# Lists of the tokens of experts two to eight: match matrices and one product in place of scatters to a table in memory

## The chip, the cores and the metric

The kernel runs on one core of a Trainium2 chip, as one program. The metric is the device time of one execution in microseconds (us), and the median of several executions is quoted. TensorE is called PE here, VectorE DVE, ScalarE ACT, GpSimd POOL; SP is the engine that issues most of the transfers. Durations of single instructions come from one profiled execution.

## The reference

Three layers follow each other: attention with two kinds of masks, a mixture of eight experts of which each token takes one, and a dense layer with a squared relu.

```
logits = x @ w_gate
e_idx = np.argmax(logits, axis=1)          # one expert per token
...
for e in range(E):
    mask = e_idx == e
    h = np.maximum(x[mask] @ w1[e], 0.0)
    ye = h @ w2[e]
    out[mask] = gate_w[mask, None] * eom[mask, e, None] * ye
...
h = np.maximum(x @ w_in, 0.0)
return (h * h @ w_out)
```

There are 2304 tokens of 512 numbers, eight experts of 512x1024x512, and a dense layer of 512x2048x512. All is float32.

## The kernel before

**Stages.** Attention runs to about 150 us, by batch and block. As it ends, tokens leave in 18 tiles of 128: each tile's rows are written to a table `x_d` in memory, and `route` finds the expert of each token and `posi`, its place in a list that gives every expert 2304 rows. Then the experts run one after the other, the largest first: the kernel calls them slots, `k` = 0 to 7, and slot `k` has `CAPS[k]` columns (416, 368, 344, ... 256). Last comes the dense layer, in three groups of six tiles, with output written by indirect transfers.

**A slot.** `e_l1(k, f)` makes a block of 128 of the 1024 inner numbers: `h` is twelve matmuls on PE. ACT takes `hh` from it (relu, rounded) and DVE `hl` (what rounding left out). `e_l2` multiplies these with the second weights: `y`, twelve matmuls a block, two blocks later. Every product of two float32 operands is three matmuls of rounded parts (`mm3`), so every weight unit of 512 KB is loaded by SP (`rw`), rounded by ACT (`hw`) and its remainder taken by DVE (`lw`, 128x1024). Five buffers hold loaded units and six hold `hw` and `lw`. In the names `hw2_0_1` the numbers are first or second weights, slot and unit.

**The tokens of a slot.** `win_load(k)` gathers the rows of slot `k` from `x_d` by an indirect transfer on POOL's queue (`win`), 128 rows at a time by a list of row numbers. `win_split` turns them on PE (`wt`), and ACT and DVE make their rounded parts `xh` and `xl`. In both orders DVE's queue holds the weight remainder `lw2_1_1` directly ahead of slot 1's first `xl1`; its buffer comes free when PE has done `y` of block 5, the last product ahead of `wt`. Slot 0's tokens and list (`lead["ix"]`) are made apart, in `match_rows` and `late_rows`, while attention ends: for each tile a 128x128 matrix says which token stands at which place modulo 128, a small operand holds tile and token number where the 128-row block is the slot's, and 13 small bfloat16 matmuls (`ips`) sum these into a list.

**The lists of slots 1 to 7.** `scatter` puts each token's number into the table `tab_d` in memory, at row `posi`: 18 indirect transfers of 128 numbers of four bytes, on POOL's queue, all after attention (`seen` holds them back until the last tile's matches are made). `rows_of` then reads a slot's list from `tab_d` into `ix`, and it waits for all scatters. The slot's expert is known from `order_slots` on DVE (`key`, `gt`, `sr`, `kk_`, `tmp`, `mf`, `meta`), which also finds offsets and surplus. `places` and 18 more indirect transfers (`idx_d`) say where each result row goes.

**What sets the order.** A scheduler lays out every engine's queue ahead of time; the engines then run their queues in that order and wait on semaphores. `tc.issue_after(x)` keeps an instruction behind `x` in that layout, and `keep_in_program_order` keeps SP's early loads in order. The parts of the weights that the dense layer needs (`e6wi`, eight-byte numbers) are loaded by SP beside the experts and converted between blocks (`conv`).

**Surplus tokens.** `overflow` handles tokens beyond `CAPS`; it stands behind a branch on `meta`, at the end.

Of the kernel before, what the change touches and what calls it, by code (L numbers as in the profile page):

```python
# [20 lines left out]
P = 128  # L21
NT = B * S
# [50 lines left out]
CONV = [(k, f) for k in range(1, 8) for f in range(8)][1:-14]  # L73
NW = (max(CAPS) + P - 1) // P
NEG = -1.0e9
# [20 lines left out]
C_TK = C_IA + P  # L96
C_END = C_TK + 2 * LATE
C_BF = C_ML - P


def make_consts():
    import numpy as np

    c = np.zeros((P, C_END), np.float32)
    p = np.arange(P)
    c[:, C_ID : C_ID + P] = np.eye(P)
    w = np.arange(KW)
    rel = (p % QB)[:, None] + STRIDE - w[None, :]
    ml = np.where((rel >= 0) & (rel < STRIDE), 0.0, NEG)
# [7 lines left out]
    c[:, C_TK:C_END:2] = np.arange(LATE)  # L117
# [14 lines left out]
def moe_kernel(ctx, tc, q, k, v, wg, wog, w1, w2, w_in64, w_out64, consts, out, dbg=None):  # L132
# [40 lines left out]
    toki = const.tile([P, NTILE, 2], I32, name="toki")  # L173
    tok1 = big.tile([P, NTILE], I32, name="tok1")

# [343 lines left out]
    late_ = []  # L519
    scat = []  # L520
    scq = []
    done = set()
# [98 lines left out]
    def match_rows():  # L621
# [9 lines left out]
        wt = wk.tile([P, LATE, 2, NW], BF16, name="wtm", tag="wtm", bufs=1)  # L631
        tk = cstb[:, C_TK - C_BF : C_END - C_BF].rearrange("p (t e) -> p t e", e=2)
        nc.vector.tensor_tensor(
# [78 lines left out]
    def late_rows(t0, t1, rows):  # L712
# [3 lines left out]
        for t in range(t0, t1):  # L716
            pm = wk.tile([P, NL], F32R, name=f"pm{t}", tag="pm", bufs=PMB)
            lead["pm"] = nc.vector.tensor_scalar(
                pm, cst[:, C_IO : C_IO + NL], rel[:, t - t0 : t - t0 + 1], None, op0=ALU.is_equal
            )  # L720
            pms.append((t, pm))
            lead["pmt"] = pm
        with tc.issue_after(lead["pm"].ins):
# [46 lines left out]
    def route(b, ts, lg, rows):  # L770
# [71 lines left out]

        def scatter(i, t):
            ins = nc.gpsimd.indirect_dma_start(  # L844
                out=tab_d[:, :],
                out_offset=bass.IndirectOffsetOnAxis(ap=posi[:, t : t + 1], axis=0),
                in_=tok1[:, t : t + 1],
                in_offset=None,
            )
            if scat:  # L850
                tc.declare_no_dep(ins.ins, group="scatter", reason="bucket rows of different tokens differ")
            tc.add_to_no_dep_group("scatter", ins.ins)
            scat.append(ins)
            return ins

        for i, t in enumerate(ts):
            scq.append(lambda i=i, t=t: scatter(i, t))

    tg = transposes(0, tiles[0])
# [6 lines left out]
    load_v(1, tiles[1])  # L866
    nc.gpsimd.memset(zero, 0)
    nc.sync.dma_start(tab_d.rearrange("(p c) o -> p (c o)", p=P), zero)
    nc.sync.dma_start(x_d[0].rearrange("(p c) -> p c", c=P), zero[: D // P, :P].bitcast(F32))
    for b in range(B):  # L870
# [60 lines left out]
    offe = r("offe", [E])  # L931

    def order_slots():
        key = r("key", [E])
# [3 lines left out]
        nc.vector.scalar_tensor_tensor(out=key, in0=lead["top"], scalar=32768.0, in1=key, op0=ALU.mult, op1=ALU.add)  # L938
        bc = lambda a: a[:, None, :].to_broadcast([P, E, E])
        bl = lambda a: a[:, :, None].to_broadcast([P, E, E])  # L940
        gt = r("gt", [E, E])
# [68 lines left out]

    def row_order_of(k):
        with tc.issue_after(lead["row"].ins):
            return nc.values_load(meta[0:1, k : k + 1], engines=[ET.Pool], min_val=0, max_val=E - 1)

    units = []
# [14 lines left out]
    def prep_unit(u):  # L1030
# [249 lines left out]
    for k in range(E):  # L1280
        for f in range(NF1):
# [188 lines left out]
    def overflow():  # L1470
# [155 lines left out]
```

## Time and profile before

| what | us |
|---|---|
| median of three executions | 814.04 (807.04 to 815.79) |
| the profiled execution | 805.34 |
| its span, first to last instruction | 803.7 |
| PE busy in it | 762.1 |
| DVE, ACT, POOL busy | 552.0, 459.4, 204.1 |

The profiled execution is 1.6 us longer than its span, and 8.7 us below the median of the three. The profile's engine shares are averages over stages: attention (to 150 us), slot 0 (150 to 209 us), slots 1 to 7 (to about 396 us) and the dense layer. PE's granted clock was 0.985 of full speed on average; where it is below 1 it is at 0.5, the lower of two levels (1.2 in place of 2.4 GHz).

### The profile page before, as it was taken

The page shows a single profiled execution, that of the slowest core. Times are in us where ns is not written, and L with a number is a line of the kernel's source. Part 1 is how long each engine was busy: PE and PEld are TensorE (multiplying, and loading weights), DVE is VectorE, ACT ScalarE, POOL GpSimd, SP SyncE. Part 2 cuts the span into 40 slices and gives each one's busy share as a digit, 9 for nine tenths or more (in the row PEclk, how much of TensorE's full clock was granted, in tenths as well). Part 3 has the DMA queues.
Part 4 walks back from the last instruction along what each step waited for, and adds up shares of the span by engine and source line. Part 5 has one row for each costly group of instructions (what it writes and reads, how often), then busy time and mean ns, then how long its engine had stood idle before and what let it go on. Part 6 is the DMA issues. An engine that isn't in the chain of part 4 may idle for free.

```text
span 803.7 us, 14547 instructions
## 1 busy us (share of the span) xinstructions
PE 762.1 (95%) x5409; PEld 681.6 (85%) x5409; DVE 552.0 (69%) x1062; ACT 459.4 (57%) x930; POOL 204.1 (25%) x193
## 2 busy tenths in 40 slices
PE   8899999993999999999999999989999999999995
PEld 4677777983999999999998889978898888899894
DVE  4777787842357587779778988897565589456533
ACT  2655646422355466566667767777565578466443
POOL 6100102744563764432013312304000003000002
PEclk9999999997899999999999999999999999999999
DMA  9799814997378998876535544454223225323002
GB/s 182 164 195 207 152 54 118 241 136 217 103 146 293 212 286 260 309 252 206 185 125 178 189 142 160 171 155 173 92 81 118 73 91 172 104 73 115 4 1 81
DMA packets 111155, 124.87 MB, mean 155 GB/s; under 512 B 40228, under 2 KB 83912, under 8 KB 111080
## 3 DMA queue, kind: packets, MB, share of 16 engines
q1 hardware_dynamic: 101256, 100.49, 46.7%
q0 software_dynamic: 8320, 22.64, 8.8%
q10 hardware_dynamic: 1504, 0.76, 0.5%
q8 instruction: 44, 0.72, 0.4%
q14 instruction: 31, 0.25, 0.1%
HBM read 101.74 MB, written 22.12 MB: 154 GB/s over the span
## 4 chain that ended last, share of the span: by engine, by line
PE 59%; issue 19%; DMA 6%; DVE 6%; POOL 5%; ACT 2%; SPq 1%; POOLq 0%; ACTq 0%; DVEq 0%
PE o L1099 5%; PE o L1100 5%; PE o L1101 5%; PE h L1099 3%; PE y L1100 3%; PE y L1099 3%; PE y L1101 3%; PE rw L551 3%; PE h L1100 3%; PE h L1101 3%; DMA tab_d<-tok,posi 2%; DMA idx_d<-toki,cpi 1%; POOL tab_d L844 1%; POOL out_dram L1361 1%; PE wt L1177 1%
## 5 line engine op out<-in xcount | busy, mean ns | idle before, releaser
L1082 DVE TENSOR_TENSOR lw<-rw,hw 128x1024 fp32r<-128x1024 f32 x62 | 79.6, 1284 | 51.8 <-ACT hw L1078 43.6
L1099 PE MATMUL o<-hwo,gh 128*128 128x512 f32 x288 | 113.8, 395 | 0.9 <-ACT gh L1331 0.9
L1100 PE MATMUL o<-lwo,gh 128*128 128x512 f32 x288 | 113.5, 394 | 0.0
L1078 ACT ACTIVATE hw<-rw 128x1024 fp32r<-128x1024 f32 x62 | 65.6, 1062 | 75.7 <-PE h L1100 51.6
L1328 ACT ACTIVATE rl<-rl 128x384 f32<-128x384 f32 x96 | 49.4, 516 | 85.4 <-DVE rl L1326 85.4
L1361 POOL DMA_INDIRECT out_dram<-ob,idx x18 | 23.6, 1311 | 251.4 <-ACT ob L1360 246.7
L1099 PE MATMUL h<-xh,hw 128*128 128x416 f32 (+7 forms) x256 | 81.3, 318 | 5.0 <-DVE hl L1206 4.9
L1101 PE MATMUL o<-hwo,gl 128*128 128x512 f32 x288 | 84.3, 396 | 0.4 <-DVE gl L1333 0.4
L1101 PE MATMUL h<-xh,lw 128*128 128x416 f32 (+7 forms) x256 | 80.1, 313 | 0.0
L1100 PE MATMUL h<-xl,hw 128*128 128x416 f32 (+7 forms) x256 | 79.9, 312 | 0.0
L1333 DVE TENSOR_TENSOR gl<-rl,gh 128x384 fp32r<-128x384 f32 x96 | 55.1, 576 | 35.0 <-ACT rl L1332 34.6
L1100 PE MATMUL y<-hl,hw 128*128 128x416 f32 (+7 forms) x256 | 77.8, 313 | 0.0
L1101 PE MATMUL y<-hh,lw 128*128 128x416 f32 (+7 forms) x256 | 77.3, 312 | 0.0
L1099 PE MATMUL y<-hh,hw 128*128 128x416 f32 (+7 forms) x256 | 66.3, 315 | 1.1 <-ACT hh L1204 1.1
L1099 PEld LDWEIGHTS o<-hwo,gh 128*128 128x128 f32 x288 | 54.1, 188 | 11.7 <-ACT gh L1331 2.2
L1100 PEld LDWEIGHTS o<-lwo,gh 128*128 128x128 f32 x288 | 54.2, 188 | 9.5
L1101 PEld LDWEIGHTS o<-hwo,gl 128*128 128x128 f32 x288 | 53.3, 188 | 9.3 <-DVE gl L1333 1.4
L1099 PEld LDWEIGHTS h<-xh,hw 128*128 128x128 f32 x256 | 48.4, 189 | 6.9 <-DVE hl L1206 6.7
L1332 ACT ACTIVATE rl<-rl 128x384 f32<-128x384 f32 x96 | 50.1, 522 | 2.2
L1331 ACT ACTIVATE gh<-rl 128x384 fp32r<-128x384 f32 x96 | 50.0, 521 | 1.9
L205 POOL TENSOR_TENSOR cvtwo<-cvtwo,cvdwo 128x512 int32<-128x512 int32 x16 | 25.6, 1607 | 94.3 <-DVE cvtwo L200 60.2
L1100 PEld LDWEIGHTS y<-hl,hw 128*128 128x128 f32 x256 | 48.8, 191 | 0.1
(614 smaller groups left out, 1935.5 us busy)
## 6 DMA issues: line engine op xcount, KB each, us to landing
rw<-in_moe_w_dram SPq DMA_DIRECT2D x62, 512.0 KB
rwa<-ws_d SPq DMA_DIRECT2D x24, 512.0 KB
rwb<-ws_d SPq DMA_DIRECT2D x24, 384.0 KB
e6wi<-in_moe_w_in_dram SPq DMA_DIRECT2D x32, 256.0 KB
rwo<-wout_d SPq DMA_DIRECT2D x16, 512.0 KB
x_d<-xr SPq DMA_DIRECT2D x18, 256.0 KB
ws_d<-eo POOLq DMA_DIRECT2D x16, 256.0 KB, 4.8
s0wo<-in_moe_w_out_dram SPq DMA_DIRECT2D x8, 512.0 KB
```

Source lines behind the costliest of these rows:

```text
L205: nc.gpsimd.tensor_tensor(t, t, rd, op=ALU.add)
L551: lead["rw"] = nc.tensor.matmul(ps[:, kk, :], xT[:, kd, col : col + P], igw[:, kd, :], start=True, stop=True)
L1078: ia = nc.scalar.activation(hi, raw, AF.Copy)
L1082: iv = eng.tensor_tensor(lo, raw, hi.bitcast(F32), op=ALU.subtract)
L1099: kept(nc.tensor.matmul(ps, ah, bh, start=first, stop=False))
L1100: kept(nc.tensor.matmul(ps, ah, bl_, start=False, stop=False))
L1101: kept(nc.tensor.matmul(ps, al, bh, start=False, stop=last))
L1328: nc.scalar.activation(rl[:, :HC], src, AF.Relu)
L1331: nc.scalar.activation(hh[:, :HC], rl[:, :HC], AF.Square)
L1332: ia = nc.scalar.activation(rl[:, :HC], rl[:, :HC], AF.Square)
L1333: iv = nc.vector.tensor_tensor(hl[:, :HC], rl[:, :HC], hh[:, :HC].bitcast(F32), op=ALU.subtract)
L1361: ins = nc.gpsimd.indirect_dma_start(out=out[:, :], out_offset=bass.IndirectOffsetOnAxis(ap=idx[:, gt_, 0:1], axis=0), in_=ob, in_offset=None,
```

## The change

The lists of slots 1 to 7 are made on the chip's engines as slot 0's list is, for all seven at once, and all scatters to `tab_d` leave the path (they stand in `overflow` now). `slot_rows` makes on DVE, from `posi` and the sorted experts, eighteen 128x128 bfloat16 match matrices (three instructions of 128x768) and an operand of 42 columns a tile (two instructions of 128x378); `end` sums eighteen matmuls of 42 columns on PE between two blocks of slot 0, and two DVE instructions make the list `rows` of 21 columns. What DVE makes lives in `y2T`, a buffer that holds results of slots later; `spots`, a load on POOL's queue, brings its constants. `order_slots` is split: what the lists need comes first, the rest (`order_rest`, `places`) after block 4. The memsets of `y2T` (`fill_sums`) come behind slot 1's gathers, and `e6wi` loads stand behind the first load of a slot-1 weight.

```diff
@@ tables, tables_end
-        nc.vector.tensor_scalar(tok1, cst[:, C_IDX : C_IDX + NTILE], 1.0, None, op0=ALU.add)
-    zero = big.tile([P, E * NT // P], I32, name="zero")
+    zero = big.tile([KD, P], F32, name="zero")
@@ before the experts
-    tab_e = tab_d.rearrange("(e r) o -> e (r o)", e=E)
-    def rows_of(k, reg):
-        ix = const.tile([P, NW], I32, name=f"ix{k}")
-        nw = (CAPS[k] + P - 1) // P
-        lead["row"] = nc.gpsimd.dma_start(ix[:, :nw], tab_e[bass.ds(reg, 1), : nw * P].rearrange("e (c p) -> p (e c)", p=P))
-        return ix
...
-        def scatter(i, t):
-            ins = nc.gpsimd.indirect_dma_start(
-                out=tab_d[:, :],
...
-    seen = wk.tile([P, 1], F32, name="seen", tag="seen", bufs=1)
-    with tc.issue_after(lead["win"].ins):
-        lead["seen"] = nc.gpsimd.tensor_copy(seen, lead["pmt"][:, 0:1].bitcast(F32))
-    with tc.issue_after(lead["seen"].ins):
-        while scq:
-            lead["row"] = scq.pop(0)()
@@ conv_load
-            nc.sync.dma_start(
...
+            with tc.issue_after(lead["w1"].ins):
+                nc.sync.dma_start(
...
@@ new
+    spots = y2T[:, 1, : C_END - C_IA]
+    nc.gpsimd.dma_start(spots, consts[:, C_IA:])
     ixs = {}
+    def slot_rows():
+        K, T = E - 1, NTILE
...
+        hi, hf, posm2, rel = new([T], I32), new([T]), new([T]), new([T, K])
+        nc.vector.tensor_scalar(hi, posi, P - 1, None, op0=ALU.bitwise_and)
+        nc.vector.tensor_copy(hf, hi)
+        nc.vector.tensor_tensor(posm2, posi, hf, op=ALU.subtract)
+        pm = y2T[:, 0, : T * P // 2].bitcast(BF16).rearrange("p (t c) -> p t c", c=P)
+        for t in range(0, T, 6):
+            sh = [P, 6, P]
+            nc.vector.tensor_tensor(
+                pm[:, t : t + 6],
+                hf[:, t : t + 6, None].to_broadcast(sh),
+                spots[:, None, :P].to_broadcast(sh),
+                op=ALU.is_equal,
+            )
+        rowb = new([E])
...
+        eq = new(sh[1:])
+        nc.vector.tensor_tensor(
+            eq,
+            rel[:, :, :, None].to_broadcast(sh),
+            cst[:, None, None, C_PJ : C_PJ + NW1].to_broadcast(sh),
+            op=ALU.is_equal,
+        )
...
+        for j in range(2):
+            nc.vector.tensor_tensor(
+                wt[:, :, j],
...
+        def end():
+            ps = psm.tile([P, 512], F32, name="rows", tag="a", bufs=6)[:, : 2 * R]
+            for t in range(T):
+                w = wt[:, t].rearrange("p j r -> p (j r)")
+                with tc.issue_after(lead["sum"].ins):
+                    nc.tensor.matmul(ps, pm[:, t], w, start=(t == 0), stop=(t == T - 1))
+            ix = const.tile([P, R], I32, name="rows")
+            nc.vector.tensor_copy(i2, ps[:, R:])
+            nc.vector.scalar_tensor_tensor(
+                out=ix, in0=ps[:, :R], scalar=float(P), in1=i2, op0=ALU.mult, op1=ALU.add
+            )
...
@@ the loop over slots and blocks
-            if f == 1 and k + 1 < E:
-                if k == 0:
-                    with tc.issue_after(lead["step"].ins):
-                        order_slots()
-                    ixs[1] = rows_of(1, row_order_of(1))
-                    fill_sums(0)
+            if (k, f) == (0, 0):
+                order_slots()
+            if (k, f) == (0, 1):
+                rows_end = slot_rows()
+            if (k, f) == (0, 3):
+                rows_end()
+            if f == (3 if k == 0 else 1) and k + 1 < E:
                 win_load(k + 1)
-                lead["row"] = lead["win"]
-                if k == 0:
-                    for d in range(1, KD):
-                        fill_sums(d)
-                if k + 2 < E:
-                    ixs[k + 2] = rows_of(k + 2, row_order_of(k + 2))
-            if (k, f) == (0, 1):
-                places()
+            if (k, f) == (0, 3):
+                for d in range(KD):
+                    fill_sums(d)
+            if (k, f) == (0, 4):
+                with tc.issue_after(lead["step"].ins):
+                    order_rest()
+                    places()
@@ overflow
+        tok1 = ov.tile([P, NTILE], I32, name="tok1")
...
+        for t in range(NTILE):
+            ins = nc.gpsimd.indirect_dma_start(
+                out=tab_d[:, :],
...
```

On POOL, from the last gather of slot 0 to what stands behind slot 1's gathers, before:

```order
L596 DMA win0_384_2051<-x_d_85,ix0_2027 32x512
L909 COPY seen_2432<-pm17_2356 128x1
L844 DMA tab_d_86<-tok1_94,posi_91 18432x1 x18
L1013 TENSOR_LOAD meta_92
L1013 ISA x2
L592 ISA
L592 DMA ix1_2586<-tab_d_86 128x3x1
L1184 MEMSET y2T_2484 128x2672
L596 DMA win1_0_2589<-x_d_85,ix1_2586 128x512
L596 DMA win1_128_2591<-x_d_85,ix1_2586 128x512
L596 DMA win1_256_2593<-x_d_85,ix1_2586 112x512
L1184 MEMSET y2T_2484 128x2672 x3
```

and now:

```order
L584 DMA win0_384_2048<-x_d_85,ix0_2024 32x512
L1156 DMA y2T_2461<-in_consts_dram 128x164
L584 DMA win1_0_2640<-x_d_85,rows_2637 128x512
L584 DMA win1_128_2642<-x_d_85,rows_2637 128x512
L584 DMA win1_256_2644<-x_d_85,rows_2637 112x512
L1153 MEMSET y2T_2461 128x2672 x4
L584 DMA win2_0_2929<-x_d_85,rows_2637 128x512
L584 DMA win2_128_2931<-x_d_85,rows_2637 128x512
```

The scatters, the reading of a register and the load of a list are gone; the load of constants stands in their place, and the first memset has moved from ahead of the gathers `win1` to behind them.

On DVE, where slot 0's first remainders `hl0_0` to `hl0_2` are taken, before:

```order
L835 TENSOR_TENSOR toki_93<-e13_2463,gsm3_2456 128x5
L836 TENSOR_TENSOR toki_93<-toki_93 128x5
L1206 SCALAR_TENSOR_TENSOR hl0_0_2528<-h0_0_2514,hh0_0_2527 128x416
L1082 TENSOR_TENSOR lw2_0_0_2500<-rw2_0_0_2496,hw2_0_0_2498 128x1024
L1206 SCALAR_TENSOR_TENSOR hl0_1_2545<-h0_1_2531,hh0_1_2544 128x416
L935 SCALAR_TENSOR_TENSOR key_2548<-cnt_2454,cst_66 128x8
L1082 TENSOR_TENSOR lw2_0_1_2506<-rw2_0_1_2502,hw2_0_1_2504 128x1024
L1206 SCALAR_TENSOR_TENSOR hl0_2_2641<-h0_2_2627,hh0_2_2640 128x416
L938 SCALAR_TENSOR_TENSOR key_2548<-top_1997,key_2548 128x8
L1082 TENSOR_TENSOR lw1_0_2_2512<-rw1_0_2_2508,hw1_0_2_2510 128x1024
```

and now (`y2T` is the place of the new lists' operands, `lw` are remainders of weight units):

```order
L1189 TENSOR_TENSOR y2T_2461<-y2T_2461 128x126
L1197 TENSOR_TENSOR y2T_2461<-y2T_2461,cst_66 128x378
L1250 SCALAR_TENSOR_TENSOR hl0_0_2506<-h0_0_2492,hh0_0_2505 128x416
L1050 TENSOR_TENSOR lw2_0_0_2478<-rw2_0_0_2474,hw2_0_0_2476 128x1024
L1181 TENSOR_TENSOR y2T_2461<-y2T_2461 128x768 x3
L1207 TENSOR_TENSOR y2T_2461<-y2T_2461 128x18x21 x2
L1050 TENSOR_TENSOR lw2_0_1_2484<-rw2_0_1_2480,hw2_0_1_2482 128x1024
L1250 SCALAR_TENSOR_TENSOR hl0_1_2536<-h0_1_2522,hh0_1_2535 128x416
L1050 TENSOR_TENSOR lw1_0_2_2490<-rw1_0_2_2486,hw1_0_2_2488 128x1024
L1250 SCALAR_TENSOR_TENSOR hl0_2_2570<-h0_2_2556,hh0_2_2569 128x416
L1050 TENSOR_TENSOR lw2_0_2_2554<-rw2_0_2_2550,hw2_0_2_2552 128x1024
L1050 TENSOR_TENSOR lw1_0_3_2654<-rw1_0_3_2650,hw1_0_3_2652 128x1024
```

New work stands ahead of `hl0_0` (its last two instructions are shown) and between the weight remainders `lw2_0_0` and `lw2_0_1`, ahead of `hl0_1`.

## Rows read from the trace of the kernel before

**Rows 1.** The page, head and part 1: span; busy time, share, instructions by engine.

```profile
span 803.7 us, 14547 instructions
...
PE 762.1 (95%) x5409; PEld 681.6 (85%) x5409; DVE 552.0 (69%) x1062; ACT 459.4 (57%) x930; POOL 204.1 (25%) x193
```

**Rows 2.** Waits of PE, whole run: engine, line, waited for: us in total, times, longest.

```profile
PE wt L1177 <- DMA win<-x_d,ix: 13.1, 1, 13.1
```

**Rows 3.** Timeline of PE, 128 to 232: start, us, engine, line, out<-in [idle before <-releaser].

```profile
133.65 0.48 PE L641 MATMUL ips<-wtm,pmh 128*128 128x8 bf16 x13
...
175.03 0.45 PE L1099 MATMUL h<-xh,hw 128*128 128x416 f32 x1 [1.80 <-DVE hl L1206]
...
199.33 1.97 PE L1177 MATMUL wt<-cst,win 128*128 128x128 f32 x8 [13.07 <-DMA win<-x_d,ix]
...
202.55 0.69 PE L1099 MATMUL y<-hh,hw 128*128 128x416 f32 x1
```

**Rows 4.** Timeline of POOL, 128 to 232, same columns.

```profile
173.95 1.37 POOL L844 DMA_INDIRECT tab_d<-tok,posi  x1 [0.30 <-issue]
188.10 0.81 POOL L592 DMA_DIRECT2D ix<-tab_d  x1 [12.78 <-DMA tab_d<-tok,posi]
...
194.45 1.04 POOL L596 DMA_INDIRECT win<-x_d,ix  x1 [3.19 <-DMA ix<-tab_d]
```

**Rows 5.** Timeline of PE, 150 to 176, same columns.

```profile
154.91 0.35 PE L1099 MATMUL h<-xh,hw 128*128 128x416 f32 x1
...
160.25 0.35 PE L1099 MATMUL h<-xh,hw 128*128 128x416 f32 x1
```

**Rows 6.** Tile tab_d: durations min/median/max in ns, first and last start; transfers' landing.

```profile
L844 POOL DMA_INDIRECT tab_d<-tok,posi x18: 967/972/2175, 145.9 to 173.9; - x18
...
DMA to landing us min/median/max: 2.5/11.2/15.6
```

**Rows 7.** Tile win, 130 to 230: the gathers' landing.

```profile
DMA to landing us min/median/max: 3.4/4.0/6.2
```

**Rows 8.** Windows: us, busy (x) by engine PE, PEld, DVE, ACT, POOL; clock, DMA, GB/s.

```profile
175.50:179.00 3.50, 3.50 (x12) 3.32 (x12) 1.23 (x1) 1.49 (x2) 0.00 (x0) 0.52 1.29 214
202.50:206.30 3.80, 3.80 (x13) 3.63 (x13) 0.79 (x2) 0.54 (x1) 3.11 (x3) 0.50 0.02 4
207.00:400.00 193.00, 189.13 (x1323) 187.22 (x1323) 137.81 (x213) 111.32 (x190) 88.43 (x90) 1.00 0.78 232
```

**Rows 9.** Waits, all engines, 130 to 240.

```profile
ACT hw L1078 <- DMA rw<-in_moe_w_dram: 21.1, 5, 8.9
```

**Rows 10.** Transfers, 168 to 173: packets and bytes moved.

```profile
DMA packets 217, 0.22 MB, mean 44 GB/s; under 512 B 4, under 2 KB 217, under 8 KB 217
```

**Rows 11.** Timeline of DVE, 128 to 232.

```profile
151.40 0.15 DVE L921 COPY cnt<-cntp 128x8 f32<-128x8 f32 x1
...
153.37 0.59 DVE L1206 SCALAR_TENSOR_TENSOR hl<-h,hh 128x416 fp32r<-128x416 f32 x1 [0.28 <-ACT hh L1204]
...
162.82 0.21 DVE L953 TENSOR_REDUCE offe<-tm 128x8 f32<-128x64 f32 x1
...
164.06 0.57 DVE L1206 SCALAR_TENSOR_TENSOR hl<-h,hh 128x416 fp32r<-128x416 f32 x1
```

**Rows 12.** Groups by form on DVE, 120 to 240: busy us, mean ns of one | idle.

```profile
L1082 DVE TENSOR_TENSOR lw<-rw,hw 128x1024 fp32r<-128x1024 f32 x18 | 22.6, 1258 | 32.2 <-ACT hw L1078 24.5 <-PE y L1101 7.7
...
L1180 DVE TENSOR_TENSOR xl<-wt,xh 128x512 fp32r<-128x512 f32 x4 | 2.7, 687 | 7.5 <-ACT xh L1179 7.5
...
L388 DVE TENSOR_TENSOR pr3l<-pr3l,rc3l 128x384 f32<-128x384 f32 x2 | 1.1, 547 | 0.0
```

**Rows 13.** Groups by form on ACT, 120 to 240.

```profile
L1078 ACT ACTIVATE hw<-rw 128x1024 fp32r<-128x1024 f32 x19 | 19.9, 1056 | 32.0 <-DMA rw<-in_moe_w_dram 21.1 <-PE h L1100 10.1 <-ACT hh L1204 0.4
```

**Rows 14.** Groups by form on POOL, whole run.

```profile
L1184 POOL MEMSET y2T<- 128x2672 f32 x4 | 9.2, 2345 | 0.0
```

**Rows 15.** Waits of ACT, 206 to 420.

```profile
ACT hw L1078 <- PE h L1100: 51.6, 22, 3.8
```

More of the change, by code (lines that the diff above doesn't have):

```diff
@@ L73 @@
 CONV = [(k, f) for k in range(1, 8) for f in range(8)][1:-14]
-NW = (max(CAPS) + P - 1) // P
+NW, NW1 = ((c + P - 1) // P for c in CAPS[:2])
 NEG = -1.0e9
@@ L96 @@
 C_TK = C_IA + P
-C_END = C_TK + 2 * LATE
+C_END = C_TK + 2 * NTILE
 C_BF = C_ML - P
@@ L116, in make_consts @@
     c[:, C_IA:C_TK] = np.arange(P)
-    c[:, C_TK:C_END:2] = np.arange(LATE)
+    c[:, C_TK:C_END:2] = np.arange(NTILE)
     c[:, C_TK + 1 : C_END : 2] = p[:, None] + 1
@@ L173, in moe_kernel @@
     toki = const.tile([P, NTILE, 2], I32, name="toki")
-    tok1 = big.tile([P, NTILE], I32, name="tok1")
     def tables():
@@ L519, in moe_kernel @@
     late_ = []
-    scat = []
-    scq = []
     done = set()
@@ L631, in match_rows @@
         wt = wk.tile([P, LATE, 2, NW], BF16, name="wtm", tag="wtm", bufs=1)
-        tk = cstb[:, C_TK - C_BF : C_END - C_BF].rearrange("p (t e) -> p t e", e=2)
+        tk = cstb[:, C_TK - C_BF : C_TK - C_BF + 2 * LATE].rearrange("p (t e) -> p t e", e=2)
         nc.vector.tensor_tensor(
@@ L721, in late_rows @@
             pms.append((t, pm))
-            lead["pmt"] = pm
         with tc.issue_after(lead["pm"].ins):
@@ L841, in route @@
             weigh()
-        def scatter(i, t):
-            ins = nc.gpsimd.indirect_dma_start(
-                out=tab_d[:, :],
[L846 to L857, printed above, removed]
     tg = transposes(0, tiles[0])
@@ L866, in moe_kernel @@
     load_v(1, tiles[1])
-    nc.gpsimd.memset(zero, 0)
-    nc.sync.dma_start(tab_d.rearrange("(p c) o -> p (c o)", p=P), zero)
-    nc.sync.dma_start(x_d[0].rearrange("(p c) -> p c", c=P), zero[: D // P, :P].bitcast(F32))
+    nc.gpsimd.memset(zero, 0.0)
+    nc.sync.dma_start(x_d[0].rearrange("(p c) -> p c", c=P), zero)
     for b in range(B):
@@ L931, in moe_kernel @@
     offe = r("offe", [E])
+    srt = {}
+    bc = lambda a: a[:, None, :].to_broadcast([P, E, E])
+    bl = lambda a: a[:, :, None].to_broadcast([P, E, E])
     def order_slots():
@@ L938, in order_slots @@
         nc.vector.scalar_tensor_tensor(out=key, in0=lead["top"], scalar=32768.0, in1=key, op0=ALU.mult, op1=ALU.add)
-        bc = lambda a: a[:, None, :].to_broadcast([P, E, E])
-        bl = lambda a: a[:, :, None].to_broadcast([P, E, E])
         gt = r("gt", [E, E])
@@ L950, in order_slots, with order_rest @@
         nc.vector.tensor_copy(meta[:, :E], mf[:, 0])
+        srt.update(gt=gt, kk=kk_)
+    def order_rest():
+        gt, kk_ = srt["gt"], srt["kk"]
         tm2 = r("tm2", [E, E])
@@ L1009, in order_of @@
         return oreg[k]
-    def row_order_of(k):
-        with tc.issue_after(lead["row"].ins):
-            return nc.values_load(meta[0:1, k : k + 1], engines=[ET.Pool], min_val=0, max_val=E - 1)
     units = []
@@ L1072, in prep_unit @@
             lead["raw"] = nc.sync.dma_start(raw, src)
+            if kind == "w1" and c == 0:
+                lead["w1"] = lead["raw"]
         nwh[0] += 1
@@ L1100, in mm3 @@
         kept(nc.tensor.matmul(ps, ah, bl_, start=False, stop=False))
-        kept(nc.tensor.matmul(ps, al, bh, start=False, stop=last))
+        lead["sum"] = kept(nc.tensor.matmul(ps, al, bh, start=False, stop=last))
     halves = [(kd, c, i) for kd, c in EARLY for i in range(2)]
@@ L1113, in conv_load @@
             s6 = w_in64[(2 * i + a) * P : (2 * i + a + 1) * P, c * UC : (c + 1) * UC].bitcast(I32)
-            nc.sync.dma_start(
-                r6.rearrange("p n t -> p (n t)").rearrange("p (j a f) -> p j a f", j=2, a=2)[:, :, a, :],
-                s6.rearrange("p (j f) -> p j f", j=2),
-            )
+            with tc.issue_after(lead["w1"].ins):
+                nc.sync.dma_start(
+                    r6.rearrange("p n t -> p (n t)").rearrange("p (j a f) -> p j a f", j=2, a=2)[:, :, a, :],
+                    s6.rearrange("p (j f) -> p j f", j=2),
+                )
         words[n] = (r6, c, i)
@@ L1182, in fill_sums, with new @@
     def fill_sums(d):
-        with tc.issue_after(lead["row"].ins):
-            lead["row"] = nc.gpsimd.memset(y2T[:, d], 0.0)
+        with tc.issue_after(lead["win"].ins):
+            nc.gpsimd.memset(y2T[:, d], 0.0)
+    spots = y2T[:, 1, : C_END - C_IA]
+    nc.gpsimd.dma_start(spots, consts[:, C_IA:])
     ixs = {}
+    def slot_rows():
+        K, T = E - 1, NTILE
+        n = [0]
+        def new(shape, dt=F32):
+            m = 1
+            for x in shape:
+                m *= x
+            a, n[0] = n[0], n[0] + m
+            assert n[0] <= NT
+            x = y2T[:, 2, a : a + m]
+            x = x if dt == F32 else x.bitcast(dt)
+            names = "abc"[: len(shape)]
+            return x.rearrange(f"p ({' '.join(names)}) -> p {' '.join(names)}", **dict(zip(names, shape)))
+        hi, hf, posm2, rel = new([T], I32), new([T]), new([T]), new([T, K])
[12 more added lines that the diff above has]
+        rowb = new([E])
+        nc.vector.tensor_scalar(rowb, mf[:, 0], float(NT), None, op0=ALU.mult)
+        nc.vector.tensor_tensor(
+            rel,
+            posm2[:, :, None].to_broadcast([P, T, K]),
+            rowb[:, None, 1:].to_broadcast([P, T, K]),
+            op=ALU.subtract,
+        )
+        sh = [P, T, K, NW1]
+        eq = new(sh[1:])
[4 more added lines that the diff above has]
+            op=ALU.is_equal,
+        )
+        R = K * NW1
+        wt = y2T[:, 3, : T * R].bitcast(BF16).rearrange("p (t j r) -> p t j r", j=2, r=R)
+        tk = spots[:, P:].rearrange("p (t j) -> p t j", j=2)
+        for j in range(2):
+            nc.vector.tensor_tensor(
+                wt[:, :, j],
+                eq.rearrange("p t k w -> p t (k w)"),
+                tk[:, :, j : j + 1].to_broadcast([P, T, R]),
+                op=ALU.mult,
+            )
+        i2 = new([R])
+        def end():
[8 more added lines that the diff above has]
+                out=ix, in0=ps[:, :R], scalar=float(P), in1=i2, op0=ALU.mult, op1=ALU.add
+            )
+            for k in range(1, E):
+                ixs[k] = ix[:, (k - 1) * NW1 : k * NW1]
+        return end
@@ L1503, in overflow @@
         tf = ov.tile([P, 3, M], F32, name="tf")
+        tok1 = ov.tile([P, NTILE], I32, name="tok1")
+        nc.vector.tensor_scalar(tok1, cst[:, C_IDX : C_IDX + NTILE], 1.0, None, op0=ALU.add)
+        none = ov.tile([P, E * NT // P], I32, name="none")
+        nc.vector.memset(none, 0)
+        nc.gpsimd.dma_start(tab_d.rearrange("(p c) o -> p (c o)", p=P), none)
+        for t in range(NTILE):
+            ins = nc.gpsimd.indirect_dma_start(
+                out=tab_d[:, :],
+                out_offset=bass.IndirectOffsetOnAxis(ap=posi[:, t : t + 1], axis=0),
+                in_=tok1[:, t : t + 1],
+                in_offset=None,
+            )
+            if t:
+                tc.declare_no_dep(ins.ins, group="scatter", reason="bucket rows of different tokens differ")
+            tc.add_to_no_dep_group("scatter", ins.ins)
         for x, add in enumerate((rowb, mf[:, 1])):
```

## The prediction

> **What bounds the kernel now.** The page's head comes first: PE is busy 762.1 us of a span of 803.7 [rows 1], so what PE waits for, and how slowly it is clocked, is nearly all there is to gain. The list of PE's waits over the whole run has one entry far above the rest: 13.1 us, once, for the gathers `win` of slot 1 [rows 2]. PE's timeline shows the place: `wt` begins at 199.33 after 13.07 idle, so the last `y` of block 5 (I call that time T) ended at 186.26 [rows 3]. The next `y` starts at 202.55.
>
> POOL's timeline, read backwards, shows why. The first gather is issued at 194.45 [rows 4], and gathers land after 3.4 to 6.2 [rows 7]; it waited for the list `ix`, issued at 188.10; that waited 12.78 for the last scatter, issued at 173.95 [rows 4]. The 18 scatters take POOL from 145.9 to 175.3, and each lands 2.5 to 15.6 after its issue, median 11.2 [rows 6].
>
> Two things hang on the same scatters. While they run, the transfers crawl: 0.22 MB in 5 us, 44 GB/s [rows 10], beside 232 GB/s over slots 1 to 7 [rows 8]. ACT waits 21.1 us for weight units, once for 8.9 [rows 9], and through ACT and DVE's queue PE stands still 1.80 us ahead of 175.03 [rows 3]. And after each idle stretch the granted clock is at the lower level: 0.52 for 3.5 us from 175.5, 0.50 for 3.8 us from 202.5 [rows 8], which cost 3.5 x 0.48 = 1.7 us and 3.8 x 0.50 = 1.9 us of work at the full level.
>
> From 207 to 400 PE is busy 189.13 of 193.00 at clock 1.00 [rows 8], and ACT's weight rounding waits 51.6 us for PE there [rows 15], so weights lie ready: a slot 1 that starts earlier carries its gain to the end.
>
> **The change, part by part.**
>
> *Removed.* The stretch from the scatters to `ix` leaves the path. The list now needs `posi`, the sorted experts, DVE, 18 matmuls and two small DVE instructions. The scatters also stop slowing the weights, so I take the 1.80 idle as gone, with the 1.7 of half clock behind it. I bound that: 0 (if the crawl has another cause) to 3.5.
>
> *DVE ahead of `hl0_0`.* Twelve small instructions, one of 126 and one of 378 columns come in. Nine small ones with up to 144 columns took 164.06-162.82 = 1.24 us, 0.14 each [rows 11]; seven of the twelve are only 8 or 18 wide, so 0.12: 1.45. I add 0.2 for the 126. The 378 is priced by the 128x384 of 547 ns [rows 12], 0.54. Sum 2.2. The ten instructions from 151.40 to 153.37 [rows 11] fill 1.4 of 1.97 us; 0.6 of waiting is there to be used, so `hl0_0` ends 1.6 later, at about 155.5. Block 2 of `h`, which started at 154.91 [rows 5], waits for it: PE loses 0.6.
>
> *DVE ahead of `hl0_1`.* Three match instructions of 768 columns: between 547 ns for 384 columns and 1258 ns for 1024 [rows 12], on the line through both 0.97. Two of 378 at 0.54. `lw2_0_1` and `hl0_1` follow, so `hl0_1` ends at 155.5 + 1.15 (`lw2_0_0`) + 2.9 + 1.1 + 1.15 + 0.55 = 162.3; block 3, at 160.25 [rows 5] and now 0.6 later, starts 1.45 late. With the match instructions at the two ends this is 0.2 to 2.3. Together PE loses 2.05; the range is 0.5 to 3.5.
>
> *PE.* The 13 small products of slot 0's list took 0.48 [rows 3], about 0.03 each, with 8 columns. 18 of 42 columns: 0.5 if the columns cost nothing, 0.8 with 34 more columns at a column per cycle of 2.4 GHz. I take 0.8. The Trainium skill, page "TensorE: Matmul & The Clock Gate", section "LDWEIGHTS (loading the stationary operand)", gives a weight load as columns / 1.2 ns, 107 ns for 128; by it the 18 would cost an estimated 1.9. The measured 13 speak against that here.
>
> *T.* 186.26 - 3.5 + 2.05 + 0.8 = 185.6.
>
> *The list and its gathers.* The products stand behind `h` of block 3 and end near 167; the copy and the last instruction have one weight remainder, 1.26 [rows 12], between them: list at about 169.5. Three gathers at 1.04 to 1.37 of POOL each [rows 4] and 3.4 to 6.2 to land [rows 7]: there by 177 to 180, six to eight us ahead of T. The four memsets, 2.345 each [rows 14], now follow the gathers; they end near 183, and the results that need them come after T. They cost nothing under that cover; without it, a part of 9.4 us. Shifting the `e6wi` loads behind the first slot-1 weight costs nothing on PE: it delays what the dense layer needs hundreds of us later. `order_rest` and `places` move behind block 4; their 18 transfers say only where outputs go.
>
> *The handover.* With the tokens there, another wait ends last. At T the buffer of slot 1's `hw2_1_1` comes free: ACT rounds it in 1.06 [rows 13], DVE's remainder takes 1.26, and only then comes the first `xl1`, 0.69 [rows 12]. The third group of `wt` needs the place of the first and waits for that. So eight `wt` run at once (1.97 at the half level [rows 3], about 1.0 at the full), PE idles about 2.0, the last four `wt` follow (half of that, 0.45 taken), and the next `y` starts at T + 1.06 + 1.26 + 0.69 + 0.45 = 189.05.
>
> *Sum.* 202.55 - 189.05 = **13.5**. If the clock also stays at the full level behind the 2.0, 1.9 more, 15.4. A wait of 1.80 brought it down before, so I take 13.5. The profiled execution took 805.34 and would take 791.8; the median of the runs is 814.04, 8.7 above it, and the median I forecast is **800.5**.
>
> **The rivals.**
>
> *B, a new wait for the gathers.* The list is made on a DVE queue behind weight remainders and its gathers ride the same transfers. If the remainder ahead of the list is late, or the gathers land after 15.6 us, the worst of the scatters, with issues of 2.17 [rows 6], the rows are there at 169.5 + 6.5 + 15.6 = 191.6 and `y` starts at about 195: gain 7.5, 806.5. For it: transfers did crawl just here. Against: the crawl goes with the scatters, and gathers landed in 6.2 at worst. Range of the gain 4 to 10. [...]
>
> *C, more gain.* The idle at the handover and both half-clock stretches vanish, or DVE's extra work costs the lower end: 17 to 20 us, 796 to 794. It needs `hw2_1_1` early, and its buffer speaks against it.
>
> *E, the change moves the wait.* PE gets to slot 1 early but then runs into weight units that before had 13 us to arrive, so that nothing is left: 814. ACT's 21.1 us of waits for units [rows 9] speak for it. Against: the crawl explains them.
>
> *D, slower.* In slots 1 to 7 the transfers are at a share of 0.78 [rows 8]; if they become the bound, PE stalls again and again. A stall such as that at 175.03 costs 1.80 + 1.7 = 3.5. To be 1% slower, 8.1 us, the 13.5 must be lost as well: 21.6 / 3.5, seven such stalls. Rows against: the largest sum of ACT's waits there is 51.6 us for PE, not for a transfer [rows 15]. With seven, 822.
>
> That the lists come otherwise than the change says is excluded by the order: no scatter and no `ix` load stands ahead of the gathers any more.
>
> **How the numbers follow.** Forecast 0.70 (gain 11.5 to 17), B 0.14, C 0.08, E 0.05, D 0.03. A measurement of this kernel tells about 1% from no change: 805.9 to 822.2 is the same. The forecast, C and a third of B are faster: 0.82; the rest of B and E the same: 0.15; D slower: 0.03. Bounds of the forecast: DVE 0.5 to 3.5, the crawl's stall 0 to 3.5, the clock 1.9. They give 10 to 17.5; with C above and the better half of B below, and some us for the median's own spread (807.04 to 815.79), **787 to 808**.
>
> **What would show it.** PE's wait for `win` is gone, and a wait of about 2 for `xl` stands at `wt`, near 186; the next `y` starts at 189. The first gather of slot 1 is issued near 169.5 and lands within 6. The match instructions take 0.9 to 1.0 each. ACT's wait for weight units falls well below 21.1, and the transfers from 157 to 172 run above 200 GB/s. The clock is 1.00 at 175 to 179. Wrong would be: `wt` still waiting for `win` (B), waits of `hw` for transfers after 190 (E, D), or an `h` that waits for `hl` by more than 3.5 in sum.

## The result, and the profile after

The changed kernel takes 788.61 us (median of 4, 786.68 to 793.55) beside 811.5 for the kernel before (4 executions, 807.04 to 815.79): a ratio of 0.9729, 95% interval 0.9665 to 0.9793. A second comparison on one chip, with more executions (e9 below), gives 789.83 (6) beside 805.64 (11), 0.9806 [0.9773, 0.9839], 15.8 us. The changed kernel's times agree; in the first comparison two of the four times of before, 814.04 and 815.79, lie above all 31 that were taken later (801.88 to 810.94). The forecast was 800.5 with a gain of 13.5, range 787 to 808, so the time lies near the fast end of the range.

The profiled execution took 793.55, 4.9 above the median. Its slot 0 begins at 152.37 instead of 150.24. So that this doesn't enter, one interval is used from here on: from the first `h` of slot 0 to the first `y` behind slot 1's `wt`. It was 202.55 - 150.24 = 52.31 us; the `y` stands in [rows 3], and the first `h` of before is this row of the same view:

```profile
150.24 0.46 PE L1099 MATMUL h<-xh,hw 128*128 128x416 f32 x1
```

The head and part 1 of the page after, which answer to [rows 1]:

```profile
span 791.7 us, 14531 instructions
...
PE 762.5 (96%) x5427; PEld 682.2 (86%) x5427; DVE 562.1 (71%) x1074; ACT 458.2 (58%) x930; POOL 173.9 (22%) x168
```

PE works as long as before; POOL lost 30 us, DVE got 10. Most of these 10 are no work but the standstill told below, which counts as busy: without it (e4) DVE has 553.7. PE's timeline after (start, us, engine, line, out<-in, idle before):

```profile
152.37 0.46 PE L1067 MATMUL h<-xh,hw 128*128 128x416 f32 x1
...
157.37 0.45 PE L1067 MATMUL h<-xh,hw 128*128 128x416 f32 x1 [0.17 <-DVE hl L1250]
...
163.67 0.46 PE L1067 MATMUL h<-xh,hw 128*128 128x416 f32 x1 [0.78 <-DVE hl L1250]
...
167.55 0.62 PE L1220 MATMUL rows<-y2T 128*128 128x42 bf16 x18
...
183.52 0.46 PE L1067 MATMUL h<-xh,hw 128*128 128x416 f32 x1 [1.52 <-DVE hl L1250]
...
187.95 1.03 PE L1146 MATMUL wt<-cst,win 128*128 128x128 f32 x8
190.94 0.95 PE L1146 MATMUL wt<-cst,win 112*128 112x112 f32 x4 [1.95 <-DVE xl L1149]
191.57 0.70 PE L1067 MATMUL y<-hh,hw 128*128 128x416 f32 x1
```

The 13.07 of [rows 3] are gone: `wt` follows `y` with no wait, and the tokens lay ready. The interval is 191.57 - 152.37 = 39.20, 13.1 less. One wait stands there that nobody had forecast: 1.52 at 183.52. Its cause is in the timelines of POOL and DVE. POOL:

```profile
170.75 0.99 POOL L584 DMA_INDIRECT win<-x_d,rows  x1 [26.39 <-DVE rows L1223]
...
173.29 0.93 POOL L584 DMA_INDIRECT win<-x_d,rows  x1 [0.30 <-issue]
174.22 9.17 POOL L1153 MEMSET y2T<- 128x2672 f32 x4
```

DVE:

```profile
158.37 2.69 DVE L1181 TENSOR_TENSOR y2T<-y2T 128x768 bf16<-128x768 f32 x3
160.97 1.01 DVE L1207 TENSOR_TENSOR y2T<-y2T 128x378 bf16<-128x378 f32 x2
...
173.54 9.88 DVE L951 CAST cpi<-cps 128x18 int32<-128x18 f32 x1
176.37 7.05 DVE L1050 TENSOR_TENSOR lw<-rw,hw 128x1024 fp32r<-128x1024 f32 x1
177.52 5.90 DVE L1250 SCALAR_TENSOR_TENSOR hl<-h,hh 128x416 fp32r<-128x416 f32 x1
```

A CAST of 18 columns lasts 9.88 us, and everything behind it in DVE's queue ends with it, at 183.42: just when POOL's four memsets end, at 183.39. The clock in stretches (columns as in [rows 8]):

```profile
170.00:180.00 10.00, 10.00 (x55) 9.93 (x54) 9.36 (x23) 3.44 (x5) 8.64 (x6) 1.00 1.07 351
...
192.00:196.00 4.00, 4.00 (x16) 3.85 (x16) 0.62 (x1) 0.47 (x1) 0.97 (x1) 0.69 0.95 272
...
207.00:390.00 183.00, 180.27 (x1272) 178.14 (x1271) 135.88 (x209) 106.07 (x181) 76.07 (x79) 1.00 0.78 237
```

Where slot 0 had a stretch at 0.52, PE now runs at 1.00 and the transfers at 351 GB/s; behind the 1.95 at `wt` the clock still falls. From 157 to 172, where the prediction looked for more than 200 GB/s, they move just 200. Slots 1 to 7 keep the gain: the dense layer's first `o` comes 252.69 us after the first `h`, 267.43 before.

### The profile page after: what moved, and what is told of

It reads as the page before. It is cut to its first block, busy times and chain, and to the rows that moved or that the text cites. A ratio compares the mean times of both kernels' runs of the same rounds, so it can differ in the third digit from the quotient of the medians.

```text
span 791.7 us, 14531 instructions
## 1 busy us (share of the span) xinstructions
PE 762.5 (96%) x5427; PEld 682.2 (86%) x5427; DVE 562.1 (71%) x1074; ACT 458.2 (58%) x930; POOL 173.9 (22%) x168
## 4 chain that ended last, share of the span: by engine, by line
PE 38%; issue 30%; DVE 6%; POOL 2%; ACT 1%; DMA 1%; ACTq 0%; POOLq 0%; DVEq 0%
PE h L1067 4%; PE h L1069 4%; PE h L1068 4%; PE y L1068 4%; PE y L1069 4%; PE y L1067 4%; PE o L1067 2%; PE o L1068 2%; PE o L1069 2%; POOL out_dram L1405 2%; DVE hl L1250 1%; PE wt L1146 1%; DVE xl L1280 1%; DVE lw L1050 1%; ACT hw L1046 1%
## 5 line engine op out<-in xcount | busy, mean ns | idle before, releaser
L1050 DVE TENSOR_TENSOR lw<-rw,hw 128x1024 fp32r<-128x1024 f32 x62 | 84.5, 1449 | 46.6 <-ACT hw L1046 39.3
L1069 PEld LDWEIGHTS y<-hh,lw 128*128 128x128 f32 x256 | 48.5, 190 | 0.1
```

Source lines behind the costliest of these rows:

```text
L1050: iv = eng.tensor_tensor(lo, raw, hi.bitcast(F32), op=ALU.subtract)
L1069: lead["sum"] = kept(nc.tensor.matmul(ps, al, bh, start=False, stop=last))
```

## The experiments

All are compared by the interval (before 52.31, changed 39.20), and by the median beside the kernel before on the same chip. Beside the first four kernels the kernel before took 807.17 (13 executions), beside e5 to e8 803.98 (7), beside e9 and e10 805.64 (11).

**e1: the scatters again, beside the new lists.**

```diff
+    with tc.issue_after(lead["win"].ins):
+        for t in range(NTILE):
+            ins = nc.gpsimd.indirect_dma_start(out=tab_d[:, :], ...posi[:, t : t + 1]..., in_=tokx[:, t : t + 1])
```

> The changed kernel with the 18 scatters to tab_d issued again on POOL after slot 0's gathers, as before; nothing reads the table, the lists come from the match matrices. Measure: from the first h of slot 0 to the first y after slot 1's wt, 39.2 us in the changed kernel (191.57 - 152.37), 52.3 before. Theory 1 (the scatters made the transfers crawl): transfers fall under 100 GB/s while they run, ACT waits for weight units 8 us or more at once again, PE stands still near 1.8 with half clock behind it, and the gathers wait on POOL's queue until the last scatter is issued: 42.5 to 48 us. Theory 2 (the crawl came from the order of the e6wi loads): the transfers stay fast, the gathers start about 8 us later and still land in time: 39 to 40.5 us.

The interval was 59.3; 802.74 us, ratio 0.995 [0.9925, 0.9975]. Both theories missed the size, through a fault of the experiment: the load of the constants fell behind the scatters. DVE's timeline of e1:

```profile
183.91 2.69 DVE L1194 TENSOR_TENSOR y2T<-y2T 128x768 bf16<-128x768 f32 x3 [16.02 <-DMA y2T<-in_consts_dram]
```

The load was issued at 170.00 and was there 13.9 us later. So the price can't be read here, but one thing can: ACT waited 13.0 us in sum for weight units, with the `e6wi` loads held back, and PE stood 1.92 at 169.84 for an `hh` behind these waits in ACT's queue. e5 repeats it in order.

**e2: only the order of the `e6wi` loads undone.**

```diff
-            with tc.issue_after(lead["w1"].ins):
+            if True:
                 nc.sync.dma_start(
```

> The changed kernel with the six e6wi loads ahead of the first slot-1 weights again, as before. Theory 1 (the scatters caused the crawl): transfers stay above 200 GB/s from 157 to 172, no wait of ACT for weights above 3 us, 39.2 us plus or minus 0.7. Theory 2 (their order caused it): ACT waits 5 to 9 us at once, PE 1.8, about 42.7 us.

790.23 us, 0.9796 [0.9758, 0.9834]; interval 41.46. ACT has no wait for weights among its waits, and the transfers run at 320 GB/s from 149 to 155. Theory 2 falls: that order caused no crawl. But the interval grew by 2.3, more than theory 1 allows, and PE's timeline puts 2.71 of waiting for `hl` at 180.81 where 1.52 stood. From 180 to 184 the granted clock is at 0.57, which adds to it. The timelines of POOL and DVE in e2 tell why:

```profile
169.35 9.16 POOL L1153 MEMSET y2T<- 128x2672 f32 x4
```

```profile
169.14 9.41 DVE L932 TENSOR_SCALAR over<-over 128x8 f32<-128x8 f32 x1
169.21 9.35 DVE L930 CAST meta<-mf 128x16 int32<-128x16 f32 x1
169.29 9.27 DVE L948 TENSOR_REDUCE cps<-cpf 128x18 f32<-128x144 f32 x1
```

The same standstill, to the memsets' end at 178.51, this time from a TENSOR_SCALAR of 8 columns, earlier in the queue, with more behind it.

**e3: what the match work costs.**

```diff
-                rows_end = slot_rows()
...
-                rows_end()
+                with tc.issue_after(lead["step"].ins):
+                    nc.vector.tensor_copy(ix[:, :NTILE], cst[:, C_IDX : C_IDX + NTILE])
```

> The changed kernel without slot_rows: no match matrices, no 18 products; the lists of slots 1 to 7 are token numbers copied from a constant at the same place in DVE's queue, so these slots get other tokens than the reference's. It prices the work that the change adds. Prediction's terms: 2.05 (DVE) + 0.8 (PE) = 2.85 less, 36.4 us. Terms read from the changed kernel's trace (idle 0.17 + 0.78 at h, and a later block 2): 1.3 + 0.6 = 1.9 less, 37.3 us. If the work hides beside something that then ends last (weights): 39.2 us.

786.26 us, 0.9742 [0.9706, 0.9777]; interval 36.61, 2.6 less. The standstill behind the memsets is there too (1.26 instead of 1.52), so some 2.3 belong to the match work: between the prediction's 2.85 and the 1.9 read from the trace.

**e4: without the CAST.**

```diff
-        nc.vector.tensor_tensor(cps, cps, posf, op=ALU.add)
-        nc.vector.tensor_copy(cpi, cps)
+        nc.vector.scalar_tensor_tensor(out=cpi, in0=cps, scalar=1.0, in1=posf, op0=ALU.mult, op1=ALU.add)
```

> The changed kernel with the CAST cpi (128x18, to int32) and the addition before it made into one SCALAR_TENSOR_TENSOR with an int32 output. In the changed kernel this CAST began at 173.54 and ended at 183.42, when POOL's four memsets of y2T (174.22 to 183.39) ended, and h waited 1.52 for hl right then. Theory 1 (the CAST is shut out while POOL works in the buffer, and DVE's queue stands behind it): DVE's instructions keep their usual 0.2, 1.2 and 0.6 us beside the memsets, the 1.52 goes, 37.7 us. Theory 2 (any DVE instruction is shut out beside the memsets): the next one, a weight remainder, stands until the memsets end, and it stays at 39.2 us.

785.45 us, 0.9743 [0.9702, 0.9784]; interval 37.15, 2.05 less. POOL's timeline of e4, then DVE's:

```profile
170.82 9.17 POOL L1152 MEMSET y2T<- 128x2672 f32 x4
```

```profile
172.97 1.23 DVE L1049 TENSOR_TENSOR lw<-rw,hw 128x1024 fp32r<-128x1024 f32 x1 [2.80 <-ACT hw L1045]
174.11 0.58 DVE L1249 SCALAR_TENSOR_TENSOR hl<-h,hh 128x416 fp32r<-128x416 f32 x1
174.84 1.23 DVE L1049 TENSOR_TENSOR lw<-rw,hw 128x1024 fp32r<-128x1024 f32 x1
```

Beside the same four memsets a remainder takes its usual 1.23, and PE's wait at that `h` is gone. Theory 2 falls, theory 1 holds. (The CASTs that were left lie ahead of the memsets, the last at 170.02: 0.14 to 0.17 each.) By the whole time e4 can't be told from the changed kernel, whose ratios were 0.9729 and 0.9806; the 2.05 is the trace's.

**e5: the scatters again, behind the constants.**

```diff
-    nc.gpsimd.dma_start(spots, consts[:, C_IA:])
+    spin = nc.gpsimd.dma_start(spots, consts[:, C_IA:])
+    with tc.issue_after(spin.ins):
+        # the 18 scatters of e1
```

> As e1, but with the load of the constants (spots) ahead of the scatters on POOL's queue, since in e1 it stood behind them and the match instructions waited 16.9 us for it. Measure as before: 39.2 us in the changed kernel from the first h to the first y after wt. Theory 1 (scatters make the transfers crawl): less than 120 GB/s from 10 to 25 us after the first h, ACT waits for weight units 13 us or so in sum as in e1, one or two stalls of PE of 1.8 with half clock, 42 to 46 us. Theory 2 (what cost the time before was only the chain scatters, table, list): the gathers are issued at most 1 to 2 us later, the interval is 39 to 40 us.

796.78 us, 0.9898 [0.987, 0.9926]; interval 47.85, beyond theory 1's 46, and theory 2 falls. Theory 1 missed two points: from 160 to 175 the transfers move 140 GB/s, not under 120, and no wait of PE ahead of `wt` reaches 1.8 (the longest is 0.90). The waits of all engines from 135 to 200 (us in total, times, longest):

```profile
ACT hw L1046 <- DMA rw<-in_moe_w_dram: 25.7, 4, 8.8
...
PE wt L1146 <- DVE xl L1149: 7.3, 1, 7.3
...
PE wt L1146 <- DMA win<-x_d,rows: 1.3, 1, 1.3
```

The transfers from 154 to 164 by queue (packets, MB, share of 16 engines), in e5:

```profile
DMA packets 238, 0.32 MB, mean 32 GB/s; under 512 B 78, under 2 KB 83, under 8 KB 238
...
q1 hardware_dynamic: 162, 0.32, 60.0%
q0 software_dynamic: 76, 0.00, 0.6%
```

and the same stretch in the changed kernel:

```profile
DMA packets 272, 0.52 MB, mean 52 GB/s; under 512 B 16, under 2 KB 16, under 8 KB 272
...
q1 hardware_dynamic: 272, 0.52, 20.7%
```

Both move little here, for few loads are issued. But the weights' queue was busy 60.0% for 0.32 MB beside the scatters and 20.7% for 0.52 MB without: 4.7 times as long for a byte. That is the extreme. From 164 to 174, with many loads, the line of this queue is, in e5:

```profile
q1 hardware_dynamic: 1484, 1.60, 103.6%
```

and in the changed kernel:

```profile
q1 hardware_dynamic: 2935, 3.16, 96.4%
```

This is 2.1 times as long for a byte, with packets of the same mean size (1.08 KB), and from 174 to 184 it is 2.2 times. The scatters' own packets take 0.6% and 1.1% in the first two stretches. This is the crawl of [rows 10], made again by 18 scatters that nobody waits for. It ends in the handover: the 7.33 at the third group of `wt` are the weight remainders ahead of `xl1` in DVE's queue, whose units came late (ACT waited 7.11 and 2.86 us for two of them).

**e6: the memsets ahead of the gathers.**

```diff
+                    for d in range(KD):
+                        nc.gpsimd.memset(y2T[:, d], 0.0)
                     win_load(k + 1)
-                for d in range(KD):
-                    fill_sums(d)
```

> The changed kernel with the four memsets of y2T (9.2 us) ahead of slot 1's gathers on POOL (and a memset of one column behind them, which keeps the order). Two questions. How much time the gathers had in hand: the prediction says 6 to 8 us before T; then wt waits for win by 1 to 4 us and the interval is 40 to 43; with more than 9 in hand it stays at 39.2. What DVE does beside the memsets: theory 1 says that the first instruction with one source (COPY, CAST or TENSOR_SCALAR) stands until the last memset ends and the queue with it, while TENSOR_TENSOR, SCALAR_TENSOR_TENSOR and TENSOR_REDUCE ahead of it keep their usual times; theory 2 (chance, another wait) says none stands.

One execution took 786.35 us, interval 37.21, 2.0 less than the changed kernel's. Slot 1's gathers, issued 173.60 to 176.19, were there when PE came to `wt` at 184.50. Counted back from `wt`, the third gather was issued 8.3 us ahead here (176.19) and 14.7 in the changed kernel (173.29), so that had at least 6.3 in hand. POOL's timeline of e6, then DVE's:

```profile
160.32 2.33 POOL L1339 MEMSET y2T<- 128x2672 f32 x1 [16.13 <-DVE y2T L1207]
166.53 4.61 POOL L1339 MEMSET y2T<- 128x2672 f32 x2 [3.88 <-PE rows L1220]
...
171.12 2.33 POOL L1339 MEMSET y2T<- 128x2672 f32 x1
```

```profile
160.18 1.22 DVE L1050 TENSOR_TENSOR lw<-rw,hw 128x1024 fp32r<-128x1024 f32 x1
...
167.35 0.17 DVE L1222 COPY y2T<-rows 128x21 f32<-128x21 f32 x1
...
170.20 3.27 DVE L946 CAST posf<-posi 128x18 f32<-128x18 int32 x1
170.28 3.20 DVE L923 TENSOR_REDUCE offe<-tm 128x8 f32<-128x64 f32 x1
```

Again the first CAST within the buffer stands until the last memset ends, at 173.45, and only then; nobody needed DVE in these 3.3 us. Theory 1 was too wide in one point: the COPY at 167.35, whose source is PE's result and not the buffer, passed beside the memsets in 0.17. That the source makes the difference is read from this one row, not tested.

**e7: slot 1's tokens ahead of its weight remainder** (on top of e4).

```diff
+        own = kind == "w2" and k == c == 1
+        if own:
+            with tc.issue_after(lead["wh"].ins):
+                ia = nc.scalar.activation(hi, raw, AF.Copy)
...
+            with tc.issue_after(lead["wl"].ins):
+                iv = eng.tensor_tensor(lo, raw, hi.bitcast(F32), op=ALU.subtract)
```

> e4 (no cast) with slot 1's xh1 and xl1 ahead of hw2_1_1 and lw2_1_1 on ACT and DVE. The prediction's step of the handover says that the third group of wt waits for 1.06 + 1.26 + 0.69 behind T; with the tokens first it is 0.5 + 0.6 + 0.69, some 1.1 us less: from 37.15 to 36.0 us. Rival: another wait (a buffer, the weights of slot 1's second unit) takes its place: 37.0 to 37.5 us.

782.81 us, 0.9737 [0.9717, 0.9758]; interval 36.23, and the wait at `wt` fell from 1.94 to 0.97. The step is as the prediction had it: the weight remainder ahead of `xl1` set the wait.

**e8: the match instructions behind `hl0_1`** (on top of e7).

```diff
+            with tc.issue_after(lead["step"].ins):
               nc.vector.tensor_tensor(
                 pm[:, t : t + 6],
```

> e7 with the three match instructions behind hl0_1 in DVE's order. In the changed kernel block 3 of h waited 0.78 for hl0_1, which stood behind them. If that is the price: 0.7 less than e7, 35.3 us. Rival: what comes behind them now is late instead (hl0_2, or the 18 products), and it is 36.0 us or more.

782.51 us, 0.9733 [0.9709, 0.9757]; interval 35.10. `h` no longer waits at block 3. By the whole time e4, e7 and e8 can't be told apart; by the trace the interval is 1.1 shorter, where the step was priced at 0.7.

**e9 and e10: the changed kernel and e8 on one chip.** No edits; e10 is e8's kernel.

> The changed kernel once more, beside e10 on one chip. Its profiled execution began slot 0 at 152.37, 2.1 us later than before, with rk waiting 1.74 us for oh. If that was one execution's accident, rk waits about 0.6 here as in six of the eight other profiles and h starts near 148 to 150.5; if it belongs to the change, 152 again. The interval from the first h to the first y after wt is 39.2 plus or minus 1. Time: 13.1 us of that interval and some 1.6 in slots 1 to 3 give 14 to 16 us, a ratio of 0.981; if the ratio of 0.973 of the first comparison holds, the other 6 us lie outside this interval.

> e8 once more on the chip of e9: interval 35.1, so 4.1 us less than the changed kernel by this interval; 785 where the changed kernel takes 789.

789.83 us (0.9806 [0.9773, 0.9839]) and 784.56 (0.9724 [0.9695, 0.9754]); intervals 38.99 and 35.11. So e8's kernel takes 5.3 us less than the changed kernel by the medians, 3.9 by the interval. From `h` to the first `o` e9 takes 251.66, 15.8 less than before's 267.43; the medians differ by 15.8 too. The two profiled executions differ by 12.2 only (805.34 and 793.17), since e9's began slot 0 2.1 later and took 1.4 more from the first `o` to its end.

`rk` waited 1.31 in e9, neither 0.6 nor 1.74, and `h` began at 152.31, which by the expectation speaks for the change. But e8 began slot 0 at 149.48 and e10, the same kernel on another chip, at 152.43 (`rk` 0.64 and 1.32), and e3 at 152.55 with `rk` at 0.60. So one kernel can begin early or late; whether the change has a part in the late start stays open.

## Why the prediction was right or wrong

The interval was forecast as 189.05 - 150.24 = 38.8 and came out at 39.2 and 39.0. Term by term:

- **The stall of 1.80 and its half clock (3.5): gone.** ACT waits for no weight unit in the changed kernel. e5 brings the crawl back, and e2 shows that the order of the `e6wi` loads alone makes none. e5 has no single stall of 1.8, but beside e4, which like e5 has no standstill behind memsets, its T comes 3.2 later after the first `h` (37.16, 33.97): near the 3.5.
- **DVE ahead of `hl0_0` and `hl0_1` (2.05): 1.29.** Block 2 came 0.33 late (5.00 after the first `h`, 4.67 before) and block 3 1.29 in all (11.30, 10.01). The 22 small instructions from 153.54 to 155.94 took 0.11 each, little less than forecast; the three match instructions took 0.90 each, not 0.97, the two of 378 columns 0.50, not 0.54. e3's 2.3 for all the match work answers to the prediction's 2.85.
- **The 18 products (0.8): 0.62.** That is 0.034 each, near the 0.03 of [rows 3]. By the rule of the Trainium skill that the prediction weighed ("TensorE: Matmul & The Clock Gate", "LDWEIGHTS (loading the stationary operand)") they would have taken an estimated 1.9; this trace, with 0.62, doesn't agree with it.
- **The memsets (0, under their cover): this step failed.** The cover hid POOL's time, but the prediction looked only for who waits for the memsets' result. DVE stood still beside them and PE paid 1.52; e4 gives it back, with 0.5 more, 0.28 of it at the handover (3.18 in e4). That the failure hardly shows in the sum is luck: DVE's and PE's terms were taken 0.9 too high.
- **The list and its gathers (6 to 8 us in hand): held.** The first gather was issued at 170.75, 18.4 after the first `h` (forecast 19.3). The changed kernel's profile shows no landing of them; in e4's they landed 3.4 to 7.2 us after their issue, 6.5 at the median, later than [rows 7] had it. `wt` still waited for nothing, and e6 shows at least 6.3 in hand.
- **The handover (T + 3.45): 3.46, and 3.18 in e9.** T came 35.74 after the first `h`, at 188.11, so it measured 191.57 - 188.11, with the forecast wait of 2.0 at 1.95 and the clock down behind it (0.69 from 192 to 196); e7 shows that `lw2_1_1` set it.
- **What was missing:** 1.6 to 2.4 us more (two profiles) came in slots 1 to 7. PE's waits there sum to 4.2 us before and to 2.8 and 1.8 in the two profiles after; for `hl` they are 3.1, 2.0 and 0.7. No experiment was made on these.

The time itself came out 11.9 below the 800.5. Most of that lies in the base: the 13.5 were taken off the median of three, 814.04, and 11 later executions of the kernel before have a median of 805.64, 8.4 lower. The gain by medians was 15.8 there, 2.3 more than forecast.

Two sums in the prediction don't come out. The bounds of the terms give a gain of 8.6 to 17.0, not 10 to 17.5; and seven stalls of 3.5 are 24.5, less the gain of 13.5 that is 825, not 822. Neither changes the forecast.

Of the rivals, B did not come: no wait for `win` but in e5, 1.3, with the scatters back. E and D did not come. C's times, 794 to 796, lie nearest the measured 788.61, but its mechanism did not come: the wait at `wt` is there with 1.95, and the clock falls behind it.

The Trainium skill's page "SBUF — State Buffer", section "Who interferes with whom", says that copy, cast and tensor_scalar can take the port pair that DVE shares with POOL, that the second to issue is blocked fully, and that a tensor_tensor has no such mode. e2, e4 and e6 agree on which instructions are held. Who came first they don't settle: the CAST of the changed kernel began 0.68 ahead of the first memset and the TENSOR_SCALAR of e2 0.21 ahead, each while POOL was still in a gather, and both waited all the same, for four memsets and not for one instruction.

How the 13.1 split: e5, with the scatters back and the lists still made on the engines, takes 8.65 more than the changed kernel. Its CASTs ran ahead of the memsets, so it pays no standstill; beside e4, which pays none either, the scatters cost 10.7. T comes 3.2 later, and the handover takes 10.69 in place of 3.18, with 1.30 for `win` and the 7.33. This second part the prediction did not see: it counted the slowed weights in T alone, and in the kernel before they lay hidden under the wait for `win`. Undone in this order, 8.65 of the 13.1 come from ending the scatters' effect on the other transfers and on POOL's queue, and 4.5 from the shorter chain to the list. Since both end at the same `wt`, the split holds for this order only; the chain kept without the crawl was not tried.

## What to carry to other kernels

Many scatters of a few bytes can cost more than their chain: look at how long the other queues take for a byte while they run. When work is moved to another place in POOL's queue, read what DVE does in the same stretch, above all its small copies and casts; a long memset is not free merely because nobody waits for its result. A wait that is taken away shows the next one in the same queue, and its price can be worked out from the order beforehand.

## What the runs showed of the hardware

- Beside POOL's memsets a CAST or TENSOR_SCALAR of 8 to 18 columns on DVE, buffer to buffer, stood 3.3 to 9.9 us (e6 and the changed kernel), until the last of several memsets had ended, not the first (9.17 us for four). TENSOR_TENSOR and SCALAR_TENSOR_TENSOR ran at their usual 1.23 and 0.58 (e4), and a COPY out of PE's result in 0.17 (e6). Beside gathers such instructions mostly passed; those that began 0.2 to 0.7 us ahead of the memsets, during the last gather, did not, and when a gather alone would hold one is left open.
- 18 scatters of 128 numbers of four bytes made the weights' queue take 2.1 to 2.2 times as long for a byte in the two busy stretches of 10 us and 4.7 times in a quiet one (e5 beside the changed kernel), with about 1% of the engines' time in their own packets. Why was not tried.
